# Cosine attention and a low-rank mixer on one core: V placed once for all row blocks, one scaling and one group's squares moved, four weight loads asked for later

## The chip, the cores and the metric

The kernel runs on one core of a Trainium2 chip. The metric is the device time of one execution in microseconds; lower is better.

## What is computed

The reference normalizes q and k along the head dimension, takes their products divided by tau = 0.1, a softmax, and the product with v. The result, with the heads side by side, goes through a mixer: a low-rank step over the sequence (U of 448x32, then V of 32x448) added to its input, and a two-layer network with relu over the channels.

```python
q_n = q / (np.linalg.norm(q, axis=-1, keepdims=True) + 1e-06)
k_n = k / (np.linalg.norm(k, axis=-1, keepdims=True) + 1e-06)
scores = np.matmul(q_n, k_n.transpose(0, 1, 3, 2)) / tau
attn = np.exp(scores - np.max(scores, axis=-1, keepdims=True))
attn = attn / (np.sum(attn, axis=-1, keepdims=True) + 1e-09)
x = np.matmul(attn, v)          # 8 batches, 12 heads, 448 rows, 64 columns
# x becomes 8 x 448 x 768; xt is x with its last two axes swapped
h = xt @ U @ V
u = x + h.transpose(0, 2, 1)
out = u + np.maximum(u @ w_ch1, 0.0) @ w_ch2     # 768 -> 3072 -> 768
```

## The kernel before

**Pairs and groups.** Two heads make a pair: 6 pairs for a batch, 48 in all, numbered n = 0 to 47. q, k and v are loaded and prepared in groups of one or two pairs, numbered from 0: the first batch has groups 0 to 3 of 1, 1, 2 and 2 pairs, each later batch has three groups of two. Group 4 is pairs 6 and 7, group 5 pairs 8 and 9, group 6 pairs 10 and 11, group 7 pairs 12 and 13, group 8 pairs 14 and 15. Three sets of staging tiles (qst, kst, vst) take turns.

**Preparing a group** (class Prep). `square` squares k or q (mostly on POOL), `reduce` sums the squares on DVE, `root` takes the square root on ACT, `invert` the reciprocal on DVE. `scale(i, j, eng)` multiplies q (i = 0) or k (i = 1) of the group's pair j by it, on DVE (V_) or POOL (P_), L259. `values` copies v in bf16 on POOL, L267. Words such as sc6q, sq4k, val3 in the order list stand for these.

**A pair's attention.** T(n) transposes the scaled q and k (on TensorE with a DVE eviction for pairs below 12, by DMA on the SP queue above), Sc makes scores on TensorE and exponentials on ACT, V multiplies by v and divides on DVE (X, L367 and L368), A and H are the two low-rank products with U and V. From pair 12 on, step_A2 and step_H2 do two pairs in one product; they use V's rows at 0, 32, 64 and 96, while pairs below 12 use one block of rows against a left operand that is zero elsewhere.

**The mixer.** For a finished batch, `steps_m1` has 24 steps f0 to f23 of six matmuls (L483), each followed by a relu on ACT (L487) or DVE (L489); `steps_m2` has the second product (L510), for two halves of the columns. These steps wait in the list `fill` and are laid between the attention steps of the next batch. f0 to f5 need the first block of w1, f6 to f11 the second, f12 to f17 the third, f18 to f23 the fourth; the second product reads w2 as four blocks, (half 0, features 0 to 11), (half 0, 12 to 23), then half 1. All eight blocks are loaded through the POOL queue with a cast.

**Order.** Every engine takes its instructions in program order; semaphores join the engines. The first batch is written out by hand in ORDER. For later pairs the loop over n lays out slots, and `put(n, i, fn)` runs fn after slot i of pair n. A slot is followed by some of the fill steps. The placing of a relu is chosen while the program is built: `Estimate` keeps a running sum of the time of PE, ACT and DVE, every step adds its price, and act_first takes the engine whose sum ends first:

```python
a = max(t["act"], t["pe"]) + act_us
d = max(t["dve"], t["pe"]) + dve_us
...
return a <= d
```

A scaling on DVE adds 0.79 to DVE's sum where it stands in the program.

**V.** Before, V is loaded once into rows 0 to 31 of V_raw at the start, and three ACT copies place it in V_sb, which was cleared. `load_copies` later loads three more row blocks, and `place_copies` places all 128 rows with three POOL copies.

Of the kernel before, what the change touches and what calls it, by code (L numbers as in the profile page):

```python
# [22 lines left out]
def kernel(  # L23
# [16 lines left out]
    nc = tc.nc  # L40
# [3 lines left out]
    R = moe_U.shape[-1]  # L44
    F = moe_w_ch1.shape[-1]
    NP = H // 2
# [69 lines left out]
    V_raw = work.tile([128, S], FP, name="V_raw", tag="XT", bufs=2)  # L116
    A_sb = [const.tile([128, 128], BF, name=f"A_sb{i}") for i in range(2)]
    V_sb = const.tile([128, S], BF, name="V_sb")
# [9 lines left out]
    def load_mixer():  # L128
        nc.gpsimd.memset(uE[:, :, S:512], 0.0)
        nc.gpsimd.memset(U_sb, 0.0)  # L130
        nc.gpsimd.memset(V_sb, 0.0)
        for t in A_sb:
            nc.gpsimd.memset(t[64:128, :], 0.0)
        nc.gpsimd.memset(U_raw[64:128, 3, :], 0.0)
        nc.gpsimd.dma_start(out=V_raw[0:R, :], in_=moe_V)
        nc.gpsimd.dma_start(out=U_raw[0:64, :, :], in_=moe_U[0:256].rearrange("(p c) r -> p c r", c=4))
        nc.gpsimd.dma_start(out=U_raw[64:128, 0:3, :], in_=moe_U[256:448].rearrange("(p c) r -> p c r", c=3))

    def place_v(copy, rows):
        lo = V_raw[rows, 0:256].rearrange("r (p c) -> r c p", c=4)  # L140
        hi = V_raw[rows, 256:448].rearrange("r (p c) -> r c p", c=3)
        body = V_sb[rows, 0:384].rearrange("r (c p) -> r c p", p=128)
        copy(out=body[:, :, 0:64], in_=lo[:, 0:3, :])
        copy(out=body[:, :, 64:128], in_=hi)
        copy(out=V_sb[rows, 384:448], in_=lo[:, 3, :])

    def place_mixer():
        nc.scalar.copy(out=U_sb[:, :, 0:R], in_=U_raw)
        place_v(nc.scalar.copy, slice(0, R))

    def load_copies():

        for r0 in (32, 64, 96):
            nc.gpsimd.dma_start(out=V_raw[r0:r0 + R, :], in_=moe_V)

    def place_copies():
        place_v(nc.gpsimd.tensor_copy, slice(0, 128))

    def load_w1(f0, f1):
        nc.gpsimd.dma_start(out=w1_sb[:, :, f0:f1],  # L160
                            in_=moe_w_ch1[:, f0:f1].rearrange("(c p) f -> p c f", p=128))

    def load_w2(half, n0, n1):
        cols = slice(half * HC, (half + 1) * HC)
        nc.gpsimd.dma_start(
            out=w2_sb[:, n0:n1, cols],
            in_=moe_w_ch2[n0 * 128:n1 * 128, cols].rearrange("(n p) d -> p n d", p=128))
# [14 lines left out]
    def load(gi, what, *engs):  # L182
        b, p0, n = groups[gi]
        engs = list(engs) * 4
        h0, nh = 2 * p0, 2 * n
        s = gi % NST

        def src(x, hs, lo, hi, c):
            return x[b, hs, lo:hi, :].rearrange("h (p c) d -> p h (c d)", c=c)

        def dst(t, ps, hs, c):
            return t[ps, hs, 0:c, :].rearrange("p h c d -> p h (c d)")

        L, U2 = slice(0, 64), slice(64, 128)
        if what == "q":
            allh = slice(h0, h0 + nh)
            engs[0].dma_start(out=dst(qst[s], L, slice(0, nh), 4), in_=src(q, allh, 0, 256, 4))  # L197
            engs[1].dma_start(out=dst(qst[s], U2, slice(0, nh), 3), in_=src(q, allh, 256, 448, 3))
            return
        x, t = (k, kst[s]) if what == "k" else (v, vst[s])  # L200
        ev, od = slice(h0, h0 + nh, 2), slice(h0 + 1, h0 + nh, 2)
        engs[0].dma_start(out=dst(t, L, slice(0, nh, 2), 4), in_=src(x, ev, 0, 256, 4))
        engs[1].dma_start(out=dst(t, U2, slice(0, nh, 2), 3), in_=src(x, ev, 256, 448, 3))
        engs[2].dma_start(out=dst(t, L, slice(1, nh, 2), 3), in_=src(x, od, 0, 192, 3))
        engs[3].dma_start(out=dst(t, U2, slice(1, nh, 2), 4), in_=src(x, od, 192, 448, 4))
# [66 lines left out]
    def by_dma(n):  # L272

        return n >= 2 * NP
# [22 lines left out]
    def step_T(b, p):  # L297
        if not by_dma(b * NP + p):
            pe_T(b, p)
            evict_T(b, p)  # L300
            return
        gi, j = group_of[(b, p)]
        nc.sync.dma_start_transpose(
            out=new_qkT(b, p).rearrange("p a (c r) -> p (a c) r", r=128),
            in_=norm[gi][0][:, j, :, :, :, :].rearrange("p i c h d -> p (i c h d)"))
# [170 lines left out]
    def steps_m1(b):  # L476
        u = u_of(b)
        o = 64 if b % 2 == 0 else 0

        def one(f):  # L480
            mp = psum.tile([128, S], FP, name="mp", tag="ps_m", bufs=2)
            for cc in range(CC):
                nc.tensor.matmul(out=mp, lhsT=w1_sb[:, cc, f * 128:(f + 1) * 128],  # L483
                                 rhs=u[:, cc, 0:S], start=(cc == 0), stop=(cc == CC - 1))
            est.pe(1.13)
            if est.act_first(0.55, 0.62):
                nc.scalar.activation(out=relu[:, f, o:o + S], in_=mp, func=AF.Relu)  # L487
            else:
                nc.vector.tensor_scalar_max(out=relu[:, f, o:o + S], in0=mp, scalar1=0.0)  # L489
            if b > 0 and f in (3, 12):  # L490
                turn(b, f // 12)

        return [lambda f=f: one(f) for f in range(NC)]
# [58 lines left out]
    preps = [Prep(gi) for gi in range(len(groups))]  # L552
    first_pair = [b * NP + p0 for b, p0, _ in groups]

    def f(n):
        for _ in range(n):
            fill.pop(0)()

    def load_all(gi):
        if gi < len(groups):  # L560
            for x in ("q", "k", "v"):
                load(gi, x, nc.sync)

    load(0, "k", nc.sync, nc.scalar)
    load(0, "q", nc.sync, nc.scalar)
    load(1, "k", nc.sync)
    load(1, "q", nc.sync)
    load(2, "k", nc.gpsimd)
    load(2, "q", nc.sync)
    load(0, "v", nc.sync)  # L570
    load(1, "v", nc.sync)
    load_mixer()

    V_, P_ = nc.vector, nc.gpsimd

    def T(n):
        step_T(*pairs[n])
# [10 lines left out]
    def Hs(n):  # L588
# [13 lines left out]
        X20 sc5q.p T4 Ac1.v ex32 Te4 V21 sc5k.p S33 X21 XT1 ex33 S40 val3 H1 ex40 A2 U1.v S41 V30  # L602
        Ac2.v ex41 S42 X30 T5 ex42 V31 Te5 S43 X31 ex43 S50 XT2 ex50 A3 S51 Ac3.v H2 V40 ex51 U2.v
        S52 X40 V41 w1_1 ex52 S53 X41 XT3 sq4q ex53 H3 A4 U3.a V50 Ac4.v XT4 X50 V51 sq4k H4 X51
        w7 U4.a A5 red4q Ac5.a XT5 H5 U5.a red4k w1_2 root4 w1_3 inv4 sc6q.v sc6k.v
    """
    bank1 = psum.tile([128, 512], FP, name="mp", tag="ps_m", bufs=2)
    spare = psum.tile([128, 512], FP, name="mp", tag="ps_m", bufs=2)
# [55 lines left out]

    for w in ORDER.split():
        word(w)
    load_w2(0, 0, 12)
    load_w2(0, 12, 24)
    preps[4].values()
    preps[4].scale(1, 1, P_)  # L670
    preps[4].scale(0, 1, V_)
    fill.extend(steps_m1(0) + steps_m2(0))
    f(3)
    T(NP)
    f(1)


    after = {}

    def put(n, at, fn):  # L680
        after.setdefault((n, at), []).append(fn)

    for gi in range(5, len(groups)):
        m, n, g = first_pair[gi], groups[gi][2], preps[gi]
        two = range(n)
        if m - 3 < NP:
            at = [(NP, 0), (NP, 6), (NP, 5), (NP, 6), (NP + 1, 0), (NP + 1, 1), (NP + 1, 2), (NP + 1, 3)]
        elif m == 2 * NP:
            at = [(m - 2, i) for i in (0, 6, 3, 4, 5)] + [(m - 1, i) for i in (0, 1, 2)]
        elif m - 3 == NP + 1:  # L690
            at = [(NP + 1, 6), (NP + 2, 5)] + [(NP + 2, i) for i in (3, 4, 5, 6)] + [(NP + 3, 0), (NP + 3, 2)]
        else:
            at = [(m - 3, 0), (m - 3, 5)] + [(m - 2, i) for i in range(6)]
        put(*at[0], lambda g=g: (g.square(1), g.square(0)))
        put(*at[1], lambda g=g: g.values())
        put(*at[2], lambda g=g: g.reduce(1))
        put(*at[3], lambda g=g: g.reduce(0))
        put(*at[4], lambda g=g: g.root())
        put(*at[5], lambda g=g: (g.invert(), [g.scale(1, j, P_) for j in two]))
        for j in two:  # L700
            put(*at[6 + j], lambda g=g, j=j: g.scale(0, j, V_))
        if gi > 5 and m - 6 <= NP:
            put(*((NP, 3), (NP + 3, 0))[gi - 6], lambda gi=gi: load_all(gi))
        elif gi > 5:
            put(m - 6, 4, lambda gi=gi: load(gi, "q", nc.sync))
            put(m - 5, 5, lambda gi=gi: load(gi, "k", nc.sync))
            put(m - 4, 3, lambda gi=gi: load(gi, "v", nc.sync))
        if by_dma(m):
            put(m - 1, -1 if m > 2 * NP else 2, lambda m=m: T(m))
            put(m - 1, 0 if m > 2 * NP else 4, lambda m=m: T(m + 1))  # L710

    put(NP, 2, lambda: (load_w2(1, 0, 12), load_w2(1, 12, 24)))
    put(NP + 3, 0, load_copies)
    put(NP + 5, 6, place_copies)

    def spread(n, order, nf, first=0):

# [14 lines left out]
    for n in range(NP, NPAIR + 1):  # L732
        b, p = pairs[n] if n < NPAIR else (B, 0)
# [115 lines left out]
```

## Time and profile before

| what | value |
|---|---|
| median of 5 runs | 595.92 us |
| lowest and highest | 595.15 and 599.01 us |
| profiled execution, its own time | 597.55 us |
| its span, first to last instruction | 595.80 us |
| mean granted TensorE clock | 0.991 |
| TensorE busy | 576.4 us, 97% of the span |
| VectorE, ScalarE, GpSimd busy | 258.0, 263.6, 190.1 us |
| DMA | 74.20 MB, 125 GB/s over the span |

The profile is of one execution, and its own time stands 1.63 us over the median of the runs. Its times count from the first instruction. In a line of the timeline the columns are the start, the duration, the engine, the line of the code, the operation, the tile written and the tile read, their shapes and the number of instructions; in brackets stand the idle time of the engine just before and what ended it. Matmul ends are modelled, so a busy TensorE is not one at its peak.

### The profile page before, as it was taken

Reading aid. Unit: us, or ns where it says so; the run is one execution under the profiler, and the core shown is the slowest. Engines: PE = TensorE matmul, PEld = TensorE weight load, DVE = VectorE, ACT = ScalarE, POOL = GpSimd, SP = SyncE. Lnnn points to the kernel's source line nnn. Section 1 sums busy time; section 2 is a strip of 40 time slices with the busy share of each in tenths; the row PEclk is TensorE's granted clock in tenths of the full one; section 3 lists DMA queues with packets and bytes.
Section 4 is the critical chain, followed back from the end, with each engine's and each line's share of the span. In section 5 each row is a group of like instructions: output and inputs, shape, how many; then the busy total and the mean of one; then the engine's idle time right before and its main releaser. Section 6 shows DMA issues by size and latency. Waiting matters only on the chain.

```text
span 595.8 us, 11562 instructions
## 1 busy us (share of the span) xinstructions
PE 576.4 (97%) x4729; PEld 328.8 (55%) x4729; DVE 258.0 (43%) x499; ACT 263.6 (44%) x452; POOL 190.1 (32%) x161
## 2 busy tenths in 40 slices
PE   6799997999999999999999999999999999999996
PEld 5564564555555545655555545555556545555564
DVE  7765665415354264633354263653355342220011
ACT  5876453336433465345443464345532465304300
POOL 9575455414053152252251351350440510000000
PEclk9999998999999999999999999999999999999999
DMA  5999999443574762673654844763636631222022
GB/s 163 202 222 234 241 240 194 120 98 87 118 140 112 166 142 75 153 172 75 133 128 114 160 124 90 156 157 87 133 98 148 140 62 28 48 65 50 5 49 54
DMA packets 138581, 74.20 MB, mean 125 GB/s; under 512 B 85568, under 2 KB 138352, under 8 KB 138528
## 3 DMA queue, kind: packets, MB, share of 16 engines
q1 hardware_dynamic: 128496, 63.06, 46.8%
q0 software_dynamic: 9728, 10.18, 10.1%
q8 instruction: 37, 0.61, 0.4%
q10 hardware_dynamic: 304, 0.21, 0.1%
q14 instruction: 16, 0.13, 0.1%
HBM read 52.19 MB, written 11.01 MB: 106 GB/s over the span
## 4 chain that ended last, share of the span: by engine, by line
PE 91%; DVE 3%; DMA 2%; SPq 1%; issue 1%; ACT 0%; POOL 0%; DVEq 0%; ACTq 0%
PE mp L510 37%; PE mp L483 36%; PE sc L318 6%; PE av L356 3%; DMA qst<-in_q_dram 2%; PE up L356 2%; DVE qk L259 2%; PE sc L312 1%; PE av L349 1%; PE tp L288 1%; PE up L349 1%; PE up L442 1%; PE av L455 1%; DVE X L368 1%; SPq L197 0%
## 5 line engine op out<-in xcount | busy, mean ns | idle before, releaser
L510 PE MATMUL mp<-w_sb,relu 128*128 128x384 bf16 x1344 | 237.7, 328 | 0.0
L510 PEld LDWEIGHTS <-relu 128*128 128x128 bf16 x1344 | 126.1, 98 | 92.9 <-issue 16.3
L483 PEld LDWEIGHTS <-w_sb 128*128 128x128 bf16 x1152 | 107.3, 98 | 100.2 <-issue 9.3
L329 ACT ACTIVATE E<-sc 128x896 bf16<-128x896 f32 x144 | 124.7, 917 | 70.6 <-PE sc L318 70.1
L487 ACT ACTIVATE relu<-mp 128x448 bf16<-128x448 f32 x166 | 90.2, 543 | 137.2 <-PE mp L483 137.1
L259 POOL TENSOR_TENSOR qk<-kst,inv 128x512 bf16<-128x512 f32 x44 | 53.0, 1222 | 266.1 <-DVE inv L253 259.7
L483 PE MATMUL mp<-uE,w_sb 128*128 128x448 bf16 x576 | 119.3, 353 | 0.0
L483 PE MATMUL mp<-uO,w_sb 128*128 128x448 bf16 x576 | 115.5, 353 | 0.0
L528 DVE TENSOR_TENSOR o_sb<-mp,ut 128x384 f32<-128x384 f32 x50 | 27.8, 556 | 122.7 <-PE mp L510 118.1
L239 DVE TENSOR_REDUCE ss<-sq 128x16 f32<-128x1024 f32 (+1 forms) x50 | 56.9, 1165 | 1.4 <-POOL sq L234 0.6
L259 DVE TENSOR_TENSOR qk<-qst,inv 128x512 bf16<-128x512 f32 x44 | 51.5, 1178 | 0.6 <-DVE inv L253 0.2
L367 DVE RECIPROCAL rd<-av 128x4 f32<-128x4 f32 x54 | 9.7, 179 | 93.8 <-PE av L356 93.8
L234 POOL TENSOR_TENSOR sq<-kst 128x1024 f32<-128x1024 f32 (+1 forms) x23 | 44.4, 1931 | 11.8 <-DMA kst<-in_k_dram 11.8
L356 PEld LDWEIGHTS <-E 128*128 128x128 bf16 x1152 | 45.4, 97 | 0.0
L234 POOL TENSOR_TENSOR sq<-qst 128x1024 f32<-128x1024 f32 x21 | 43.3, 2060 | 0.0
L318 PE MATMUL sc<-qkT 64*128 64x448 bf16 x288 | 42.0, 360 | 0.9 <-ACT E L326 0.3
L326 ACT ACTIVATE E<-sc 128x448 bf16<-128x448 f32 x48 | 25.9, 540 | 32.9 <-PE sc L312 32.9
L267 POOL CAST v<-vst 128x1024 bf16<-128x1024 f32 (+1 forms) x25 | 29.0, 1161 | 14.2 <-DMA vst<-in_v_dram 9.7
L489 DVE TENSOR_SCALAR relu<-mp 128x448 bf16<-128x448 f32 x26 | 16.2, 622 | 30.7 <-PE mp L483 30.3
L356 PE MATMUL av<-v,E 128*128 128x65 bf16 x648 | 29.1, 193 | 0.0
L349 PEld LDWEIGHTS <-E 128*128 128x128 bf16 x192 | 18.0, 98 | 18.2 <-issue 2.9
L367 DVE RECIPROCAL rd<-up 128x4 f32<-128x4 f32 x36 | 6.5, 181 | 45.0 <-PE up L356 45.0
(93 smaller groups left out, 322.5 us busy)
## 6 DMA issues: line engine op xcount, KB each, us to landing
out_dram<-o_sb SPq DMA_DIRECT2D x112, 96.0 KB, 2.2
w_sb<-in_moe_w_ch_dram POOLq DMA_DIRECT2D x8, 1152.0 KB, 26.5
qst<-in_q_dram SPq DMA_DIRECT2D x23, 256.0 KB, 4.0
vst<-in_v_dram SPq DMA_DIRECT2D x46, 128.0 KB, 2.8
kst<-in_k_dram SPq DMA_DIRECT2D x44, 128.0 KB, 2.7
qst<-in_q_dram SPq DMA_DIRECT2D x23, 192.0 KB, 4.1
vst<-in_v_dram SPq DMA_DIRECT2D x46, 96.0 KB, 2.6
kst<-in_k_dram SPq DMA_DIRECT2D x44, 96.0 KB, 2.7
```

What stands on the lines that cost most here:

```text
L234: nc.gpsimd.tensor_mul(sq[:, 0:self.nh * 4, :], self.flat(t), self.flat(t))
L239: nc.vector.reduce_sum(self.ss[:, j, 0:self.nh * 4], self.sq[j][:, 0:self.nh * 4, :], axis=AX.X)
L259: eng.tensor_mul(qks[self.gi % 2][:, j, i, :, :, :], t[:, 2 * j:2 * j + 2, :, :].rearrange("p h c d -> p c h d"), iv.unsqueeze(3).to_broad ...
L267: nc.gpsimd.tensor_copy(out=self.flat(v65[self.s])[:, :, 0:D], in_=self.flat(vst[self.s]))
L318: nc.tensor.matmul(out=sc[:, h, 0:S], lhsT=t[r, 1, c * 128:(c + 1) * 128], rhs=t[r, 0, 0:S], start=True, stop=True)
L329: nc.scalar.activation(out=e[:, 2 * c:2 * c + 2, 0:S], in_=sc[:, :, 0:S], func=AF.Exp)
L349: nc.tensor.matmul(out=av[:, i, :, :], lhsT=e[:, 6, ic * 128:(ic + 1) * 128], rhs=vv[:, 2 * j:2 * j + 2, 3, :], start=(i == 0), stop=False ...
L356: nc.tensor.matmul(out=av[:, i, h, :], lhsT=e[:, 2 * c + h, ic * 128:(ic + 1) * 128], rhs=vv[:, 2 * j + h, c, :], start=False, stop=(i == ...
L483: nc.tensor.matmul(out=mp, lhsT=w1_sb[:, cc, f * 128:(f + 1) * 128], rhs=u[:, cc, 0:S], start=(cc == 0), stop=(cc == CC - 1))
L487: nc.scalar.activation(out=relu[:, f, o:o + S], in_=mp, func=AF.Relu)
L510: nc.tensor.matmul(out=mp, lhsT=relu[:, f, r0:r0 + 128], rhs=w2_sb[:, f, half * HC:(half + 1) * HC], start=(f == 0), stop=(b > 0 and f == ...
L528: nc.vector.tensor_add(o.rearrange("p (k d) -> p k d", d=128), mp.rearrange("p (k d) -> p k d", d=128), ut_of[(b, half)][:, :, c, :])
```

## The change

V is loaded into all four row blocks at the start, two blocks through the ACT queue and two through the POOL queue, and the three ACT copies place all 128 rows at once; the clearing of V_sb, the later loads and the later copies go. The k scaling of pair 7 on POOL stands behind the first three fill steps and the transposes of pair 6; its q scaling on DVE stands behind slot 1 of pair 6, after f4. The last two blocks of w1 and the first two of w2 are asked for behind f3 instead of ahead of it. The squares of group 8 are put at slot 4 of pair 11 instead of slot 0.

```diff
--- before.py
+++ after.py
@@ -128,33 +128,23 @@
     def load_mixer():
         nc.gpsimd.memset(uE[:, :, S:512], 0.0)
         nc.gpsimd.memset(U_sb, 0.0)
-        nc.gpsimd.memset(V_sb, 0.0)
         for t in A_sb:
             nc.gpsimd.memset(t[64:128, :], 0.0)
         nc.gpsimd.memset(U_raw[64:128, 3, :], 0.0)
-        nc.gpsimd.dma_start(out=V_raw[0:R, :], in_=moe_V)
+        for r0 in (64, 96):
+            nc.gpsimd.dma_start(out=V_raw[r0:r0 + R, :], in_=moe_V)
         nc.gpsimd.dma_start(out=U_raw[0:64, :, :], in_=moe_U[0:256].rearrange("(p c) r -> p c r", c=4))
         nc.gpsimd.dma_start(out=U_raw[64:128, 0:3, :], in_=moe_U[256:448].rearrange("(p c) r -> p c r", c=3))
 
-    def place_v(copy, rows):
-        lo = V_raw[rows, 0:256].rearrange("r (p c) -> r c p", c=4)
-        hi = V_raw[rows, 256:448].rearrange("r (p c) -> r c p", c=3)
-        body = V_sb[rows, 0:384].rearrange("r (c p) -> r c p", p=128)
-        copy(out=body[:, :, 0:64], in_=lo[:, 0:3, :])
-        copy(out=body[:, :, 64:128], in_=hi)
-        copy(out=V_sb[rows, 384:448], in_=lo[:, 3, :])
-
     def place_mixer():
+
+        lo = V_raw[:, 0:256].rearrange("r (p c) -> r c p", c=4)
+        hi = V_raw[:, 256:448].rearrange("r (p c) -> r c p", c=3)
+        body = V_sb[:, 0:384].rearrange("r (c p) -> r c p", p=128)
         nc.scalar.copy(out=U_sb[:, :, 0:R], in_=U_raw)
-        place_v(nc.scalar.copy, slice(0, R))
-
-    def load_copies():
-
-        for r0 in (32, 64, 96):
-            nc.gpsimd.dma_start(out=V_raw[r0:r0 + R, :], in_=moe_V)
-
-    def place_copies():
-        place_v(nc.gpsimd.tensor_copy, slice(0, 128))
+        nc.scalar.copy(out=body[:, :, 0:64], in_=lo[:, 0:3, :])
+        nc.scalar.copy(out=body[:, :, 64:128], in_=hi)
+        nc.scalar.copy(out=V_sb[:, 384:448], in_=lo[:, 3, :])
 
     def load_w1(f0, f1):
         nc.gpsimd.dma_start(out=w1_sb[:, :, f0:f1],
@@ -563,6 +553,8 @@
 
     load(0, "k", nc.sync, nc.scalar)
     load(0, "q", nc.sync, nc.scalar)
+    for r0 in (0, 32):
+        nc.scalar.dma_start(out=V_raw[r0:r0 + R, :], in_=moe_V)
     load(1, "k", nc.sync)
     load(1, "q", nc.sync)
     load(2, "k", nc.gpsimd)
@@ -602,7 +594,7 @@
         X20 sc5q.p T4 Ac1.v ex32 Te4 V21 sc5k.p S33 X21 XT1 ex33 S40 val3 H1 ex40 A2 U1.v S41 V30
         Ac2.v ex41 S42 X30 T5 ex42 V31 Te5 S43 X31 ex43 S50 XT2 ex50 A3 S51 Ac3.v H2 V40 ex51 U2.v
         S52 X40 V41 w1_1 ex52 S53 X41 XT3 sq4q ex53 H3 A4 U3.a V50 Ac4.v XT4 X50 V51 sq4k H4 X51
-        w7 U4.a A5 red4q Ac5.a XT5 H5 U5.a red4k w1_2 root4 w1_3 inv4 sc6q.v sc6k.v
+        w7 U4.a A5 red4q Ac5.a XT5 H5 U5.a red4k root4 inv4 sc6q.v sc6k.v
     """
     bank1 = psum.tile([128, 512], FP, name="mp", tag="ps_m", bufs=2)
     spare = psum.tile([128, 512], FP, name="mp", tag="ps_m", bufs=2)
@@ -664,15 +656,16 @@
 
     for w in ORDER.split():
         word(w)
-    load_w2(0, 0, 12)
-    load_w2(0, 12, 24)
     preps[4].values()
-    preps[4].scale(1, 1, P_)
-    preps[4].scale(0, 1, V_)
     fill.extend(steps_m1(0) + steps_m2(0))
     f(3)
     T(NP)
+    preps[4].scale(1, 1, P_)
     f(1)
+    load_w1(1536, 2304)
+    load_w1(2304, 3072)
+    load_w2(0, 0, 12)
+    load_w2(0, 12, 24)
 
 
     after = {}
@@ -691,7 +684,7 @@
             at = [(NP + 1, 6), (NP + 2, 5)] + [(NP + 2, i) for i in (3, 4, 5, 6)] + [(NP + 3, 0), (NP + 3, 2)]
         else:
             at = [(m - 3, 0), (m - 3, 5)] + [(m - 2, i) for i in range(6)]
-        put(*at[0], lambda g=g: (g.square(1), g.square(0)))
+        put(*((NP + 5, 4) if m == 2 * NP + 2 else at[0]), lambda g=g: (g.square(1), g.square(0)))
         put(*at[1], lambda g=g: g.values())
         put(*at[2], lambda g=g: g.reduce(1))
         put(*at[3], lambda g=g: g.reduce(0))
@@ -709,9 +702,8 @@
             put(m - 1, -1 if m > 2 * NP else 2, lambda m=m: T(m))
             put(m - 1, 0 if m > 2 * NP else 4, lambda m=m: T(m + 1))
 
+    put(NP, 1, lambda: preps[4].scale(0, 1, V_))
     put(NP, 2, lambda: (load_w2(1, 0, 12), load_w2(1, 12, 24)))
-    put(NP + 3, 0, load_copies)
-    put(NP + 5, 6, place_copies)
 
     def spread(n, order, nf, first=0):
```

## The prediction

> **What bounds the kernel now.** I read the page's busy shares first, then stretches one clock window long, then the timeline wherever the diff touches it. Groups and pairs count from 0; f4 is step 4 of the first product; sc7k is the scaling of pair 7's k.
>
> ```profile
> PE 576.4 (97%) x4729; PEld 328.8 (55%) x4729; DVE 258.0 (43%) x499; ACT 263.6 (44%) x452; POOL 190.1 (32%) x161
> ```
>
> TensorE is the bound: a gap opened in it is paid in full, and only its idle time can be won. The stretches (length, PE busy, instructions, granted clock, DMA share, GB/s) show what idling costs beside itself:
>
> ```profile
> 58.96:62.37 3.41, 2.19 (x18) 1.00 1.23 239
> ...
> 96.51:99.92 3.41, 1.31 (x15) 0.99 0.79 183
> 99.92:103.33 3.41, 2.47 (x14) 0.50 0.75 143
> 103.33:106.75 3.42, 3.42 (x13) 0.51 0.57 151
> ```
>
> A window with 1.22 us idle kept the clock; one with 2.10 us idle was followed by two at half clock. Next, the timeline around the moved scalings:
>
> ```profile
> 44.91 1.49 POOL L259 TENSOR_TENSOR qk<-kst,inv 128x512 bf16<-128x512 f32 x1 [2.13 <-DVE inv L253]
> 45.41 1.55 DVE L259 TENSOR_TENSOR qk<-kst,inv 128x512 bf16<-128x512 f32 x1
> ...
> 46.87 0.68 DVE L259 TENSOR_TENSOR qk<-qst,inv 128x512 bf16<-128x512 f32 x1
> ...
> 49.18 1.31 PE L483 MATMUL mp<-uE,w_sb 128*128 128x448 bf16 x6
> ...
> 50.33 0.61 PE L288 MATMUL tp<-ident,qk 128*128 128x128 bf16 x8
> ...
> 50.84 0.56 ACT L487 ACTIVATE relu<-mp 128x448 bf16<-128x448 f32 x1
> ...
> 52.06 1.89 POOL L234 TENSOR_TENSOR sq<-kst 128x1024 f32<-128x1024 f32 x1 [5.66 <-DMA kst<-in_k_dram]
> ```
>
> sc7q (46.87, the line that moves) is done 2.8 us before its reader, the transposes of pair 7 at 50.33. Those don't wait. POOL reaches group 5's squares at 52.06, because kst lands then. And sc6k takes 1.55 us instead of sc7q's 0.68 because sc7k holds it off until 46.40. POOL's queue ahead of that:
>
> ```profile
> 38.02 1.70 POOL L160 DMA_DIRECT2D w_sb<-in_moe_w_ch_dram  x2
> 39.71 2.03 POOL L165 DMA_DIRECT2D w_sb<-in_moe_w_ch_dram  x2
> 41.71 1.07 POOL L267 CAST v<-vst 128x1024 bf16<-128x1024 f32 x1
> ```
>
> These are the four weight loads that move. Last, the place of group 8's squares, and the same arrangement one group later:
>
> ```profile
> 95.52 1.89 POOL L234 TENSOR_TENSOR sq<-kst 128x1024 f32<-128x1024 f32 x1
> 95.62 4.63 DVE L259 TENSOR_TENSOR qk<-qst,inv 128x512 bf16<-128x512 f32 x2
> ...
> 100.86 0.59 PE L389 MATMUL av<-X,U_sb 128*128 128x128 bf16 x4 [3.03 <-DVE X L368]
> ```
> ```profile
> 113.97 2.74 DVE L259 TENSOR_TENSOR qk<-qst,inv 128x512 bf16<-128x512 f32 x2
> 116.12 2.34 POOL L234 TENSOR_TENSOR sq<-kst 128x1024 f32<-128x1024 f32 x1
> ```
>
> Two DVE scalings that take 0.68 us each alone take 4.63 us beside two squares; X behind them is late, and TensorE waits 3.03 us.
>
> [...]sc6k ends 0.56 us after sc7k, and 4.63 us holds both squares. [...] The trace agrees, with the bound between 1.39 us idle (the window from 4.35, clock kept) and 2.10. [...] Summing the trace's packets, the load queue moved about 150 KB per 2 us beside weight traffic and 500 without.
>
> **The change, part by part.**
>
> *V.* POOL at the start loses one memset (0.50) and gains one DMA issue (0.51): +0.01. ACT gains two issues behind its own q load (ends 2.92), at about 0.6 like its others, ending near 4.15; its first squares start at 4.14. At most +0.1, and the next squares wait for DMA 0.24 anyway. 112 KB more among the first loads: up to +0.2. The ACT copies keep shape and 1.29 us (POOL's 128-partition twins took 1.25 against ACT's 32-partition ones); they ran 3.6 us after V landed. At 76.5 POOL loses 1.56 us of issues, at 106 it loses 1.25 us of casts; neither had a waiting reader. Sum: 0 to +0.3, I take +0.1.
>
> *Weight loads.* POOL is in order. Now val4 comes first, then sc7k, which waits for inv4 until 44.76 as before; so its start and sc6k's delay stay. Queued behind it are the four loads, starting near 46.4 (+8.4) and ending 3.7 later at 50.1. The weight queue had emptied at 43.6 and took 1.5 us from issue to first packet (33.41 to 34.9), so it stands empty 43.6 to 47.9: later blocks land at most 4.3 later. Landings were about 52.9, 60.8, 70.9 and 81.0; readers begin at 63.79 (f12), 74.62 (f18), 84.84 and 88.43. The tightest keeps 3 us. Cost 0, covered by that; without cover up to 4.3. The gap lets the load queue move about 0.75 MB early, so kst of group 5 lands near 47 and of group 6 near 57 rather than 66.
>
> *The planner.* Every relu goes to ACT or DVE by the code's running sums. sc7q adds 0.79 to DVE's sum; taken behind f4, two relus change sides: f4 goes to DVE (its sums 31.94 against 31.15) and f6 to ACT (32.49 against 33.25). These are the code's sums, not times.
>
> *sc7q behind f4.* DVE is in order. f4's matmuls end at 50.33, its relu runs about 50.5 to 51.1, and only then can sc7q start. But POOL begins group 5's squares at 50.1, since kst is there[...]. sc7q ends 0.56 later, at 52.6, and pair 7's q transposes, due at 50.55, wait about **2.1 us**. Bounds: 1.2 if sc7q gets in first (51.1 + 0.68), 2.9 if it meets a square just begun. f5 and everything on TensorE is queued behind. What is then late: f6's relu now stands before an exponential on ACT, whose score buffer the next matmuls wait for (0.34 already): **+0.3**.
>
> *Group 6's squares.* They waited 3.35 us for kst, until 66.14. With it landed they follow sc9k at 62.79, 0.2 ahead of sc9q:
>
> ```profile
> 62.97 0.68 DVE L259 TENSOR_TENSOR qk<-qst,inv 128x512 bf16<-128x512 f32 x1
> ...
> 64.92 0.39 PE L389 MATMUL av<-X,U_sb 128*128 128x128 bf16 x4
> ...
> 66.14 1.89 POOL L234 TENSOR_TENSOR sq<-kst 128x1024 f32<-128x1024 f32 x1 [3.35 <-DMA kst<-in_k_dram]
> ```
>
> sc9q would end at 62.79 + 1.89 + 0.56 = 65.2, X at 65.85, and the matmul of 64.92 waits **0.95 us** (0 if sc9q wins).
>
> *Group 8's squares.* On POOL nothing lies between their old and new places in program order, so they still start when the two k scalings end. The lines at 113.97 and 116.12 show it: those squares stand behind the DVE scalings in the program, and started while the second ran. Cost 0.
>
> *Clock.* 2.1 us of idle lies in one window with more than about 1.75 (middle of the bounds) in (3.41 - 2.1 + 0.7)/3.41 = 59% of phases; a window at half speed loses about 1.5 us. I take +0.7.
>
> Sum: 0.1 + 2.1 + 0.3 + 0.95 + 0.7 = 4.15. The profiled execution took 597.55 (span 595.80 and 1.75 around it), 1.63 over the median of 595.92; it would become 601.7, the median 600.1, rounded to **600.0**.
>
> **Rivals.** (1) *The collisions mostly miss* (0.30): [...]the clock holds: +1.6, near 597.5. For it: 0.2 us decides at 62.8. Against: POOL is a whole microsecond ahead at 50.1.
> (2) *Faster* (0.07): group 8's squares do fall behind the scalings at 95.62. Then these end near 97.1, X is in time, and TensorE keeps 3.03 us plus half of the 5.89 us that it was busy at half clock, 2.95: 590 where sc7q costs nothing, 593.4 beside its 3.45. It decides if the squares start 1.6 us later than 95.52; if DVE merely wins by 0.1 us, 1.3 is gained. Against: the 116.12 line.
> (3) *Weights late* (0.05): f12 or the second product waits up to 4.3 more: 604. Against: 3 us or more to spare.
> (4) *The change does less than it says*: for the squares' move that is my forecast already.
> My forecast holds 0.58.
>
> **How the numbers follow.** 0.5% is 3 us, about what a measurement of this kernel can tell from no change. Forecast and (3) give slower, 0.63; (1), and a forecast with the low ends, give 0.30 within; (2) 0.07. The likeliest case alone spans 598.5 to 602. Downward the range takes in (1) and a DVE win at 95.6: 595.5; upward the 2.9 bound with a lost clock window and a part of (3): 603.
>
> **What would show it.** Right: f4's relu on DVE, sc7q starting after 51 and ending near 52.6, a wait of about 2 us at pair 7's transposes for DVE; group 5's squares near 50.1 without a DMA wait; weight loads from 46.4; sc9q near 2 us; squares still directly behind the k scalings at the 95.5 place with the 3 us wait. Wrong: pair 7's transposes without a wait, or scalings of 0.7 us and no half clock there.

## The result, and the profile after

| | before | after |
|---|---|---|
| median | 595.69 us (47 runs) | 599.01 us (28 runs) |
| lowest and highest | 593.28 and 599.01 us | 594.22 and 602.47 us |
| profiled execution, its own time | 597.55 us | 594.65 us |
| its span, mean granted clock | 595.80 us, 0.991 | 592.9 us, 0.998 |

The ratio of the times is 1.0050, with a 95% interval of 1.0036 to 1.0064: slower by 3.3 us, right at the half per cent that the prediction takes for the least that can be told from no change. Runs more than 1.5% above the fastest of their kernel count as slow and enter no ratio: one of 3318.62 us in the second set of after, and three (603.03 to 603.35 us) of the exchange of group 5's squares. The two profiled executions say the opposite, since chance picked an execution of before 1.9 us over its median, with two stretches at half clock, and one of the fastest of after. So the profile of after is read here for places and waits, not for its total.

The page of after, busy time by engine:

```profile
PE 574.0 (97%) x4729; PEld 328.2 (55%) x4729; DVE 258.5 (44%) x499; ACT 263.4 (44%) x452; POOL 188.5 (32%) x155
```

TensorE is still the bound. POOL has 6 instructions fewer. The code lines of after stand 10 lower than those of before (L249 is before's L259, L473 its L483). The stretches of after (length, busy time and count of each engine, granted clock, DMA share, GB/s), at the times where before lost its clock:

```profile
96.51:99.92 3.41, 1.33 (x15) 0.82 (x12) 3.41 (x2) 0.75 (x2) 3.41 (x3) 1.00 0.81 155
99.92:103.33 3.41, 2.46 (x21) 1.59 (x20) 0.86 (x3) 0.26 (x1) 1.25 (x1) 1.00 0.75 142
```

The idling is before's to 0.02 us (1.33 us busy, 1.31 before), yet the clock stays at 1.00: the same gap costs a clock window in one execution and none in another. The times at which the clock changes in a trace tell where they differ. From its first record of the clock at 4.27 on, before keeps one clock for 23.893, 3.413, 68.267, 6.827 and 488.106 us, which is 7, 1, 20, 2 and 143 times 3.413 us; after, from 7.09 on, for 583.679 us, 171 times. Stretches of 3.413 us counted from a change are called windows here. In before the clock rises at 106.67 and next falls at 594.78, 143 windows on. Cut at their edges, before has

```profile
96.43:99.84 3.42, 1.40 (x18) 0.89 (x15) 3.42 (x2) 0.82 (x2) 3.42 (x3) 1.00 0.79 185
99.84:103.26 3.42, 2.40 (x14) 1.54 (x14) 0.92 (x3) 0.26 (x1) 1.30 (x1) 0.50 0.75 142
```

and after, whose clock falls only at 590.77, 144 windows behind an edge at 99.25, has

```profile
95.84:99.25 3.41, 2.00 (x26) 1.39 (x24) 3.41 (x2) 1.02 (x2) 3.41 (x2) 1.00 0.91 168
99.25:102.66 3.41, 1.79 (x17) 1.27 (x17) 1.53 (x3) 0.26 (x1) 1.92 (x2) 1.00 0.75 141
```

In before one window holds 2.02 us of idle time, and the clock falls at its end. In after an edge splits the same gap into 1.41 and 1.62 us. The timeline of after around the moved scalings (start, us, engine, line, operation, the idle time ahead of it and what ended it):

```profile
42.59 1.50 POOL L249 TENSOR_TENSOR qk<-kst,inv 128x512 bf16<-128x512 f32 x1 [2.29 <-DVE inv L243]
...
43.09 1.55 DVE L249 TENSOR_TENSOR qk<-kst,inv 128x512 bf16<-128x512 f32 x1
...
44.03 1.70 POOL L150 DMA_DIRECT2D w_sb<-in_moe_w_ch_dram  x2
...
45.73 2.03 POOL L155 DMA_DIRECT2D w_sb<-in_moe_w_ch_dram  x2
...
47.82 1.89 POOL L224 TENSOR_TENSOR sq<-kst 128x1024 f32<-128x1024 f32 x1
48.01 0.39 PE L278 MATMUL tp<-ident,qk 128*128 128x128 bf16 x4
48.21 0.62 DVE L479 TENSOR_SCALAR relu<-mp 128x448 bf16<-128x448 f32 x1 [2.17 <-PE mp L473]
48.75 1.50 DVE L249 TENSOR_TENSOR qk<-qst,inv 128x512 bf16<-128x512 f32 x1
49.67 2.33 POOL L224 TENSOR_TENSOR sq<-qst 128x1024 f32<-128x1024 f32 x1
50.31 0.40 PE L278 MATMUL tp<-ident,qk 128*128 128x128 bf16 x4 [1.91 <-DVE qk L249]
...
54.04 0.37 PE L308 MATMUL sc<-qkT 64*128 64x448 bf16 x2 [0.58 <-ACT E L316]
```

sc7k and sc6k (42.59 and 43.09) are as before. The four weight loads follow at 44.03 and 45.73. Group 5's squares begin at 47.82 with no wait, f4's relu runs on DVE (48.21), sc7q (48.75) takes 1.50 us instead of 0.68 since it starts inside the first square, and the q transposes of pair 7 wait 1.91 us. The second place, group 6's squares and sc9q:

```profile
62.97 2.44 POOL L224 TENSOR_TENSOR sq<-kst 128x1024 f32<-128x1024 f32 x1 [0.17 <-DMA kst<-in_k_dram]
...
62.99 0.68 DVE L249 TENSOR_TENSOR qk<-qst,inv 128x512 bf16<-128x512 f32 x1
```

They start 0.02 us apart. Here the DVE scaling took its 0.68 us, although its recorded start is the later one, and the square took 2.44 us instead of 1.89. And the place of group 8's squares, with the next group's after it:

```profile
95.53 1.89 POOL L224 TENSOR_TENSOR sq<-kst 128x1024 f32<-128x1024 f32 x1
95.64 4.63 DVE L249 TENSOR_TENSOR qk<-qst,inv 128x512 bf16<-128x512 f32 x2
...
100.87 0.38 PE L379 MATMUL av<-X,U_sb 128*128 128x128 bf16 x4 [3.03 <-DVE X L358]
...
111.20 2.74 DVE L249 TENSOR_TENSOR qk<-qst,inv 128x512 bf16<-128x512 f32 x2
```

Nothing has changed at the first: same start, same 4.63 us, same wait of 3.03 us.

### The profile page after: what moved, and what is told of

Read it like the earlier page. It is cut to its first block, busy times and chain, and to the rows that moved or that the text cites. A ratio compares the mean times of both kernels' runs of the same rounds, so it can differ in the third digit from the quotient of the medians.

```text
span 592.9 us, 11556 instructions
## 1 busy us (share of the span) xinstructions
PE 574.0 (97%) x4729; PEld 328.2 (55%) x4729; DVE 258.5 (44%) x499; ACT 263.4 (44%) x452; POOL 188.5 (32%) x155
## 4 chain that ended last, share of the span: by engine, by line
PE 92%; DVE 3%; ACT 2%; DMA 2%; issue 1%; SPq 0%; DVEq 0%; ACTq 0%
PE mp L500 37%; PE mp L473 36%; PE sc L308 6%; PE av L346 3%; PE up L346 2%; DVE qk L249 1%; PE sc L302 1%; PE av L339 1%; DMA qst<-in_q_dram 1%; ACT E L319 1%; PE tp L278 1%; PE up L339 1%; PE up L432 1%; DMA kst<-in_k_dram 1%; PE av L445 1%
## 5 line engine op out<-in xcount | busy, mean ns | idle before, releaser
L473 PEld LDWEIGHTS <-w_sb 128*128 128x128 bf16 x1152 | 107.3, 98 | 100.2 <-issue 9.3
L249 POOL TENSOR_TENSOR qk<-kst,inv 128x512 bf16<-128x512 f32 x44 | 53.0, 1222 | 277.1 <-DVE inv L243 267.4
L473 PE MATMUL mp<-uE,w_sb 128*128 128x448 bf16 x576 | 119.3, 353 | 0.0
L473 PE MATMUL mp<-uO,w_sb 128*128 128x448 bf16 x576 | 115.6, 353 | 0.0
L249 DVE TENSOR_TENSOR qk<-qst,inv 128x512 bf16<-128x512 f32 x44 | 52.4, 1197 | 0.7 <-DVE inv L243 0.2
```

What stands on the lines that cost most here:

```text
L249: eng.tensor_mul(qks[self.gi % 2][:, j, i, :, :, :], t[:, 2 * j:2 * j + 2, :, :].rearrange("p h c d -> p c h d"), iv.unsqueeze(3).to_broad ...
```

## The experiments

The theory behind them is the prediction's: sc7q, later on DVE, meets group 5's squares, which are earlier because of the weight loads, and TensorE waits. The rivals are that sc7q's own later place is enough, that the weight loads or V cost something themselves, and that POOL's issuing of DMAs, not its squares, holds DVE. Beside each median stands its ratio to before on the same chip, with the 95% interval. Gains in us are differences of medians. The ratios put some of them lower: 1.7 us for the weight loads alone instead of 2.3, and 4.4 from after to sc7q put back instead of 5.3.

**The V part alone, in before.**

```diff
+    for r0 in (0, 32):
+        nc.scalar.dma_start(out=V_raw[r0:r0 + R, :], in_=moe_V)
...
-    put(NP + 3, 0, load_copies)
-    put(NP + 5, 6, place_copies)
```

> The kernel before with V's part of the change alone (four loads at the start, placed once, no clearing, no later loads or copies). Theory 1 (the moved q scaling costs the time): first squares on ACT start near 4.8 instead of 4.14 as in the changed kernel, the first batch up to 1 us later, nothing at the transposes of pair 7; 595.7 to 596.7. Rival (V's loads cost the time): all of the 3.3 us, near 599.

Measured: 595.68 us, ratio 0.9997 (0.9982 to 1.0012, 14 runs). V costs nothing that can be measured. Its trace also shows the order before in an execution whose first batch was not late, as that of the profile of before was:

```profile
52.41 1.89 POOL L224 TENSOR_TENSOR sq<-kst 128x1024 f32<-128x1024 f32 x1 [8.16 <-DMA kst<-in_k_dram]
```
```profile
57.99 1.30 PE L473 MATMUL mp<-uE,w_sb 128*128 128x448 bf16 x6 [1.15 <-DVE relu L479]
60.88 0.40 PE L278 MATMUL tp<-ident,qk 128*128 128x128 bf16 x4 [1.41 <-POOL qk L249]
```

POOL waits 8.16 us for group 5's kst. The squares end late, DVE's reductions behind them and then its relu are late, and a step of the first product waits 1.15 us, the transposes of pair 8 then 1.41. The same two waits stand in the trace of before with group 8's squares really moved (below): 0.84 us at 58.36 and 1.37 at 61.22. In the profile of before the first is absent: its first batch ran some 2.2 us late (pair 6's eviction starts at 47.67, here at 45.51; a wait of 2.22 us for v stands at 27.62), so that kst had come when it was needed.

**sc7q's move alone, in before.**

```diff
-    preps[4].scale(0, 1, V_)
     fill.extend(steps_m1(0) + steps_m2(0))
...
+    put(NP, 1, lambda: preps[4].scale(0, 1, V_))
```

> The kernel before with pair 7's q scaling alone moved behind f4; weight loads, V and squares as before. Theory 1: f4's relu on DVE, the scaling behind it from about 51.1, but the squares of group 5 are not yet there (kst lands at 52), so it takes 0.7 and the transposes of pair 7 wait about 1.2 us, plus 0.3 at a score product; near 597.2, more where a clock window is lost. Rival (the order costs nothing without the early squares, or the time comes from V): 595.7.

Measured: 595.74 us, ratio 1.0009 (0.9995 to 1.0022, 14 runs). In its trace pair 7's transposes do wait, 1.09 us at 49.75, and sc7q takes 0.68 us because the squares only come at 52.24. The waits of 1.15 and 1.41 us, seen above, are 0 and 1.06 here: the planner's other choice for the relus took one wait away while it made another. The late place alone is not what costs 3.3 us.

**The four weight loads alone, in before.**

```diff
-        ... red4k w1_2 root4 w1_3 inv4 sc6q.v sc6k.v
+        ... red4k root4 inv4 sc6q.v sc6k.v
...
-    load_w2(0, 0, 12)
-    load_w2(0, 12, 24)
...
     T(NP)
     f(1)
+    load_w1(1536, 2304)
+    load_w1(2304, 3072)
+    load_w2(0, 0, 12)
+    load_w2(0, 12, 24)
```

> The kernel before with the four weight loads alone asked for behind f3. Theory 1: POOL is in order, the loads leave at about 46.4 and all blocks land before their readers; group 5's squares start near 50 instead of 52 with no reader hurried; 595.7, within 0.5. Rival (weights late): a wait at f12 or at the second product, up to 4.3 us, 600.

Measured: 593.34 us, ratio 0.9971 (0.9954 to 0.9988, 22 runs): a gain of 2.3 us. Its profiled execution was its slowest, 600.44 us, and shows only what can go wrong in it:

```profile
48.79 2.40 DVE L259 TENSOR_TENSOR qk<-qst,inv 128x512 bf16<-128x512 f32 x1
```
```profile
48.26 1.70 POOL L160 DMA_DIRECT2D w_sb<-in_moe_w_ch_dram  x2
49.96 2.03 POOL L165 DMA_DIRECT2D w_sb<-in_moe_w_ch_dram  x2
51.98 1.93 POOL L234 TENSOR_TENSOR sq<-kst 128x1024 f32<-128x1024 f32 x1
```

sc7q takes 2.40 us while POOL does nothing but issue DMAs. What held it there was not isolated.

**After, with sc7q put back.**

```diff
+    preps[4].scale(0, 1, V_)
     fill.extend(steps_m1(0) + steps_m2(0))
...
-    put(NP, 1, lambda: preps[4].scale(0, 1, V_))
```

> The changed kernel with pair 7's q scaling alone put back ahead of the first three steps (V, weight loads, pair 7's k scaling and squares stay changed). Theory 1: f4's relu is back on ACT, the transposes of pair 7 do not wait, 2.2 us and most of the lost clock windows are won back: 595.5 to 596.8. Rival (V or the weights cost the time): it stays near 599.

Measured: 593.69 us, ratio 0.9976 (0.9957 to 0.9996, 15 runs). This one edit takes 5.3 us from after. Its trace, of one of its faster executions (592.33 us), tells where the weight loads' gain lies:

```profile
44.58 0.68 DVE L249 TENSOR_TENSOR qk<-qst,inv 128x512 bf16<-128x512 f32 x1
```
```profile
47.80 1.90 POOL L224 TENSOR_TENSOR sq<-kst 128x1024 f32<-128x1024 f32 x1
```
```profile
59.08 0.40 PE L278 MATMUL tp<-ident,qk 128*128 128x128 bf16 x4 [1.06 <-POOL qk L249]
```

The squares begin at 47.80, 4.6 us ahead of the V experiment's; the 1.15 us wait is gone and that of pair 8 is 1.06 instead of 1.41. That makes 1.5 of the 2.3 us; the rest was not traced. sc7q is long done.

**After itself, once more.**

> The changed kernel once more, beside the others on one chip, to see what the 5.3 us between it and the kernel with the q scaling put back consist of. The wait at pair 7's transposes with what follows it makes 2.2 us. Theory 1: the rest is clock windows that this wait costs in most executions; 598 to 600, and profiles that hold half-clock windows show them just behind 48 to 52 us. Rival (the first runs met a different state of the first loads): near 596, no windows there.

Measured: 598.73 us, ratio 1.0061 (1.0038 to 1.0083, from 16 of the 17 runs, whose median is 598.53). The profiled execution took 602.75 us, at a clock of 0.988. DVE, POOL and TensorE in it:

```profile
48.91 3.33 DVE L249 TENSOR_TENSOR qk<-qst,inv 128x512 bf16<-128x512 f32 x1
...
67.38 2.21 DVE L249 TENSOR_TENSOR qk<-qst,inv 128x512 bf16<-128x512 f32 x1
```
```profile
47.91 1.92 POOL L224 TENSOR_TENSOR sq<-kst 128x1024 f32<-128x1024 f32 x1
49.76 1.91 POOL L224 TENSOR_TENSOR sq<-qst 128x1024 f32<-128x1024 f32 x1
```
```profile
52.29 0.61 PE L278 MATMUL tp<-ident,qk 128*128 128x128 bf16 x4 [3.74 <-DVE qk L249]
...
70.20 0.38 PE L379 MATMUL av<-X,U_sb 128*128 128x128 bf16 x4 [0.70 <-DVE X L358]
```

sc7q is recorded from 48.91, within the first square, which ended at 49.83; the second ran from 49.76 to 51.67, and sc7q ended at 52.24, 0.6 us after both. TensorE waited 3.74 us, and the transposes then took 0.61 us where they take 0.40 at full clock. Cut at the clock's steps:

```profile
47.17:50.58 3.41, 1.38 (x10) 0.70 (x8) 2.22 (x2) 1.63 (x3) 3.41 (x3) 1.00 1.14 216
50.58:54.00 3.42, 1.71 (x8) 1.01 (x9) 2.72 (x3) 0.00 (x0) 3.42 (x4) 0.50 1.14 238
54.00:57.41 3.41, 3.41 (x11) 1.21 (x8) 1.88 (x2) 0.54 (x1) 0.72 (x1) 0.50 1.15 234
```

The clock fell at 50.58, when TensorE had idled for 2.03 us and the wait had 1.7 us still to go, and came back at 57.41. At 67.38 the second collision is there, too: sc9q takes 2.21 us and TensorE waits 0.70.

**f4's relu left on ACT.** The planner's 0.79 for sc7q is booked where it was before; sc7q itself stays at its later place.

```diff
-            if eng is nc.vector:
+            if eng is nc.vector and not (self.gi == 4 and j == 1):
                 est.dve(0.79)
...
+    est.dve(0.79)
     fill.extend(steps_m1(0) + steps_m2(0))
```

> The changed kernel, with the 0.79 of pair 7's q scaling booked in the planner's sums where it was booked before, and the scaling itself left behind slot 1 of pair 6. Theory 1 (the planner's flip is what puts the scaling late): f4's relu returns to ACT, the scaling runs right behind the eviction of pair 6, no wait at pair 7's transposes; 593 to 595. Rival (the scaling's place alone is late): it stays near 599.

Measured: 593.66 us, ratio 0.9966 (0.9949 to 0.9982, 22 runs), as if sc7q had not been moved. In its trace sc7q runs from 46.14 for 0.68 us, directly behind the eviction of pair 6, and pair 7's transposes don't wait; f6's relu is back on DVE as well. In the trace of after DVE idled 2.17 us ahead of f4's relu, although the reciprocals that sc7q reads had been ready since 42.44, and sc7q ran only behind that relu. So what hurts is not the line to which sc7q was moved, but that a relu for which DVE idles 2.17 us until f4's matmuls end stands ahead of it on DVE, and that this relu is on DVE only because of the running sum.

**Group 5's squares exchanged with the last two w2 loads on POOL.**

```diff
-            at = [(NP, 0), (NP, 6), ...
+            at = [(NP, 2), (NP, 6), ...
...
-    put(NP, 2, lambda: (load_w2(1, 0, 12), load_w2(1, 12, 24)))
+    put(NP, 0, lambda: (load_w2(1, 0, 12), load_w2(1, 12, 24)))
```

> The changed kernel with group 5's squares and the last two w2 loads exchanged on POOL, so that the first square starts some 2 us later. Theory 1[...]: the scaling behind f4 meets no square and takes 0.7, the transposes of pair 7 wait 1.1 instead of 1.9, and fewer clock windows are lost; 596 to 598. Rival (the scaling is late by DVE's order alone, or the issue of a DMA on POOL holds it as a square does): wait 1.9 or more, 599.

Measured: 596.67 us, ratio 1.0026 (1.0004 to 1.0048, from 19 of the 22 runs, whose median is 596.00), in two clusters, 13 runs of 593.65 to 597.6 and 9 of 599.7 to 603.4. The profiled execution (603.31 us) is near the top of the second:

```profile
48.78 5.34 DVE L249 TENSOR_TENSOR qk<-qst,inv 128x512 bf16<-128x512 f32 x1
```
```profile
45.75 4.04 POOL L155 DMA_DIRECT2D w_sb<-in_moe_w_ch_dram  x4
49.78 1.94 POOL L224 TENSOR_TENSOR sq<-kst 128x1024 f32<-128x1024 f32 x1
51.63 1.93 POOL L224 TENSOR_TENSOR sq<-qst 128x1024 f32<-128x1024 f32 x1
```

With two microseconds less of overlap planned, the hold is longer: sc7q stands through the last microsecond of the DMA issues and both squares. The median is what theory 1 expected, but this trace is not: the issues seem to hold DVE as well, here and in the weight experiment. How sc7q fares in the faster cluster was not seen.

**Group 5's squares on ACT.** After, with these two squares taken from POOL; the planner's sums are left as they were.

```diff
-        put(..., lambda g=g: (g.square(1), g.square(0)))
+        put(..., lambda g=g: (g.square(1, g.gi == 5), g.square(0, g.gi == 5)))
```

> The changed kernel with group 5's two squares on ACT, in an idle stretch of it, and not booked in the planner's sums, so that no relu moves. POOL then issues the last two w2 loads where the squares ran. Theory 1[...]: the scaling behind f4 takes 0.7, the transposes wait 1.1, 595 to 596.5 with few clock windows. Rival[...]: the scaling takes over 1 us in a part of the executions, waits of 1.5 to 3, 596.5 to 598. Rival (DVE's order alone costs the time): 599.

Measured: 595.33 us, ratio 0.9982 (0.9970 to 0.9994, 22 runs). DVE and POOL:

```profile
48.73 0.68 DVE L250 TENSOR_TENSOR qk<-qst,inv 128x512 bf16<-128x512 f32 x1
```
```profile
45.71 4.05 POOL L155 DMA_DIRECT2D w_sb<-in_moe_w_ch_dram  x4
```

sc7q takes 0.68 us with POOL issuing all the while, so an issue does not always hold DVE; pair 7's transposes wait 1.09 us.

**The same, with those two w2 loads behind slot 2 of pair 7**, so that POOL does nothing beside sc7q.

```diff
-    put(NP, 2, lambda: (load_w2(1, 0, 12), load_w2(1, 12, 24)))
+    put(NP + 1, 2, lambda: (load_w2(1, 0, 12), load_w2(1, 12, 24)))
```

> As the run with group 5's squares on ACT, with the last two w2 loads also behind slot 2 of pair 7, so that POOL does nothing while the scaling behind f4 runs. Theory 1: the scaling takes 0.7 in every execution, the transposes wait 1.1, 594.5 to 596; what remains over the kernel with the scaling put back (593.7) is DVE's order alone, 1.1 and 0.3. Rival (DVE's order alone costs the time): 599.

Measured: 595.66 us, ratio 0.9983 (0.9970 to 0.9996, 22 runs); the trace has 0.68 and 1.09 us again. The two agree: over many executions the issues cost nothing here, the squares do. With the squares on ACT none of 22 runs goes above 596.5 us, though POOL issues the same loads then as in the exchange, where 9 of 22 stand at 599.7 or more.

**Group 8's squares really moved, in before**, ahead of the k scalings rather than behind them, at slot 4 of pair 10, with the copy of v one slot later.

```diff
-        put(*at[0], lambda g=g: (g.square(1), g.square(0)))
-        put(*at[1], lambda g=g: g.values())
+        early = m == 2 * NP + 2
+        put(*((NP + 4, 4) if early else at[0]), lambda g=g: (g.square(1), g.square(0)))
+        put(*((NP + 4, 5) if early else at[1]), lambda g=g: g.values())
```

> The kernel before with the squares of group 8 moved the other way, to slot 4 of pair 10, and its v copy to slot 5, so that POOL does them ahead of group 7's k scalings. Theory 1: nothing on POOL meets group 7's q scalings near 95.6, the 3.03 us wait for X at 100.9 goes and with it half-clock windows behind it; 590 to 592.5. Rival (X is late for another reason, or POOL's k scalings become late instead): 594 to 596.

Measured: 592.71 us, ratio 0.9953 (0.9937 to 0.9969, 12 runs), the fastest of all.

```profile
95.46 2.15 DVE L259 TENSOR_TENSOR qk<-qst,inv 128x512 bf16<-128x512 f32 x2
...
98.21 0.38 PE L389 MATMUL av<-X,U_sb 128*128 128x128 bf16 x4 [0.55 <-DVE X L368]
```

The two scalings take 2.15 us instead of 4.63 and TensorE waits 0.55 us instead of 3.03. This is the gain that the change's words speak of and that its diff does not reach. Of the change's own move of these squares no run was made: the code puts nothing else on POOL between the two slots, so with that one line as before the instructions of all five engines stand in the very same order as in after.

**The two gains together**, the weight loads and these squares, in before.

> The kernel before with two things: the four weight loads behind f3 (as in the run of the weight loads alone) and group 8's squares and v copy ahead of group 7's k scalings (as in the run of the early squares). If the two gains (2.3 and 3.0 us) have different causes they add: 590 to 591.5. If both came from the same clock windows: 592.5.

Measured: 594.42 us, ratio 0.9972 (0.9958 to 0.9986, 22 runs): they don't add up. TensorE, and when the two DMA transposes into qkT landed, counted from their issue:

```profile
95.94 0.38 PE L389 MATMUL av<-X,U_sb 128*128 128x128 bf16 x4 [0.55 <-DVE X L368]
...
101.51 0.55 PE L318 MATMUL sc<-qkT 64*128 64x448 bf16 x4 [2.85 <-DMA qkT<-qk]
```
```profile
DMA to landing us min/median/max: 6.9/7.2/7.4
```

The wait for X is 0.55 us, as hoped, and a new one of 2.85 us stands 5.6 us later: pairs 14 and 15 are transposed by DMA, and these two transposes landed 6.9 and 7.4 us after their issue, against 3.9 and 4.5 where the squares alone were moved and 3.1 in before. They are issued earlier (from 94.01, not 96.28) while the weight queue, delayed by the other part, still runs: between 96 and 98 us it moved 0.43 MB and the queue of the transposes a single packet; by 100 to 102 it was down to 0.02 MB. That the late weights are the reason is how the trace reads and is not shown; no run with that traffic elsewhere was made.

## Why the prediction was right, and where it was not

It said 600.0 us, slower; measured were 599.01 here and 598.53 in the second set. To compare its terms I use one more reckoning: a run's time multiplied by its mean granted clock, roughly what it would take at full clock. Medians of these products:

| kernel | product, us |
|---|---|
| before | 593.0 |
| V alone | 592.9 |
| weight loads alone | 591.6 |
| after, sc7q put back | 591.8 |
| after, group 5's squares on ACT | 592.9 |
| after | 595.6 |

The product counts idle time at half clock as half, so it is too low where a clock window was lost. Executions with a mean clock of 1.000 need no such reckoning and agree roughly: 592.30 and 592.92 us with sc7q put back, 595.58, 595.97 and 598.00 for after.

*V, +0.1.* Right: 0 within the interval. The first squares on ACT began at 4.81 instead of 4.14, behind the two V loads, whose issue ended at 4.68 and not at 4.15, and the first transposes came 0.35 us later.

*Weight loads, 0.* This step failed, by -2.3 us. It looked for lateness and found none, rightly; but it took the profile of before for a usual execution. There the late first batch had hidden what the late kst costs: in the V experiment 1.15 us for the relu and 0.35 more at pair 8. The prediction itself had kst landing 5 us earlier, and asked what that would collide with, not what it would relieve.

*T(7), +2.1, bounds 1.2 and 2.9.* That sc7q meets the squares was right, and the size of the wait was not one number. The order on DVE alone gives 1.09 (squares on ACT), one square 1.91, both squares 3.74, which lies above the upper bound. The bound held that a square just begun is the worst that can be met; that was an estimate, and it counted one square. It put sc7q's end 0.56 us behind that square's, as sc6k ended 0.56 us behind sc7k in before. In after sc7q, begun within the first square, did end 0.54 us behind it; in the trace of 3.33 us it ended 2.41 us behind the first and 0.57 us behind the second, so that a scaling can be held by the next square as well. Between the squares on ACT and after lie 595.6 - 592.9 = 2.7 us of product; the longer hold would be 3.74 - 1.09 = 2.65, the shorter 0.82. So the longer seems the usual one; how often each falls is not shown.

*The score product, +0.3.* 0.58 instead of 0.34: 0.24.

*Group 6's squares against sc9q, +0.95, or 0 if sc9q wins.* Both were seen: 0 in the profile of after, 0.70 in the second. That kst would land near 57 was wrong (near 62.8), so that POOL's lead was not the 0.2 us expected: with 0.02 us (62.97 to 62.99) sc9q took 0.68 us, and with 0.21 in the second trace (67.17 to 67.38) 2.21 us.

*Group 8's squares, 0.* Right: 95.53, 4.63 and 3.03 are unchanged. The rival of a faster kernel rested on DVE's getting in first, and neither trace of after shows it.

*The clock, +0.7.* Too small. From the kernel with sc7q put back to after the time rises by 5.3 us and the product by 3.8, which leaves some 1.5 for the clock. The prediction put the bound at about 1.75 us idle within a window. That was an estimate, the middle between 1.39 us in before's window from 4.35, which kept the clock, and 2.10; so was its 1.5 us for a window, from the 5.89 us that TensorE was busy in before's two windows at half clock. In windows cut at the clock's steps it lies nearer 2.0: the wait of 1.91 us in after lay whole in the window from 48.05 and kept the clock, as did 1.96 us with the squares on ACT (window from 98.07), while 2.02 us in before and 2.03 in the second trace of after lost it. The bound is not sharp, since two windows of the first batch lost the clock with less: 1.65 us (weight loads alone, from 23.26) and 1.79 us (group 8's squares moved, from 5.95). With 2.0, and every phase of the windows as likely, a wait of 2.1 us would lose the clock in some 44% of phases instead of 59, one of 1.91 in none, and one of 3.74 in some 92%; this is an estimate from those figures. By that estimate it is the longer hold that brings the clock's cost with it. In the two windows that lost it with 2.02 and 2.03 us idle TensorE was busy for 1.40 and 1.38 us, so a window need not be wholly idle to lose the clock.

The prediction's sum, 4.15, stands against 3.3. With the terms as the runs gave them, and the longer hold: 0 - 2.3 + 3.7 + 0.24 + 0.7 + 1.5 = 3.8; with the shorter hold and sc9q ahead, 0 - 2.3 + 1.9 + 0.24 = -0.2, without a loss of clock from that wait. The measured median lies between, nearer the first. So the number was near for a reason that was partly luck: an unseen gain of 2.3 us on one side, and on the other a wait too small by up to 1.6 and a clock term too small by some 0.8, nearly made each other up.

## What to carry to other kernels

A profile is one execution: before a wait of zero is taken from it, look whether something earlier ran late in that execution, since lateness upstream hides what is late downstream. An operation moved behind a late one on its engine is to be checked against the whole run of work on the engine beside which it was seen to slow, not against one instruction of it: sc7q took 0.68 us with the squares on ACT, and with them on POOL 1.50 in one execution and 3.33 in another. When two edits each bring forward the same stretch, look whether its transfers can come forward too: here the second edit seems only to have moved the wait.

## What the hardware showed that I had not expected

- A DVE scaling that starts within a GpSimd square does not always end just behind it: in one execution it ended 0.54 us behind the first of two squares (1.50 us in all), in another 0.57 us behind the second (3.33 us), by the same program. What decides is open.
- While GpSimd did nothing but issue DMAs, the same scaling, sc7q, took 2.40 us in one trace, and in another it stood through the last microsecond of such issues and two squares (5.34 us); in four others with such issues under way it took 0.68 us. What decides is open.
- Two DMA transposes landed 3.1 us after their issue where the weight queue moved 0.10 MB or less in 2 us, 3.9 and 4.5 us beside 0.32 MB, and 6.9 and 7.4 us beside 0.30 to 0.43 MB. The amount alone does not tell these apart.
- The wait of 3.03 us for X lost the clock in before and kept it in after, where a window's edge split the idle time into 1.41 and 1.62 us. Of all windows cut at the clock's steps, 1.96 us was the most idle time that kept the clock and, the first batch apart, 2.02 the least that lost it.
